# Attention-state scan with a gated MLP on one core: late steps in another order, a 128-row identity product, U in pairs

## The chip, the cores and the metric

One core of a Trainium2 chip. The time is that of the device for one execution, in microseconds; the median of several runs counts. Engines: TensorE (PE, with its weight loads as PEld), VectorE (DVE), ScalarE (ACT), GpSimd (POOL), SyncE (SP), which issues most DMAs. Each engine runs its own queue in order and waits on semaphores of the others.

## What is computed

For each of 4 batches and 8 heads a 40x40 state runs over 768 tokens; the outputs are joined and go through a gated MLP. Cut to what matters:

```python
for t in range(S):
    y[:, :, t] = einsum('bhd,bhde->bhe', rt, state)
    Sa = einsum('bhde,bhe->bhd', state, at)
    state = state * wt - outer(Sa, bt) + outer(vt, kt)
x = y with the heads joined                    # 4 x 768 x 320
h = relu(x @ w_in); u, v = halves of h         # 512 columns each
v = normalized over its 512 columns
out = (u * (w_spatial @ v + b_spatial)) @ w_out
```

All is float32. The matrices of the MLP are split into two parts, a high one and a rest, so one product becomes three.

## The kernel before, in words

**Two phases.** `phase1` does the scan and, beside it, the first layer of the MLP; `phase2` does the spatial product (L179 to L181) and the last product (L199). In phase 1 the tokens go in chunks of 64. There are 24 steps (`NS`): two pairs of batches, 12 chunks each; a step handles 2 batches by 8 heads, that is 8 units (`NU`) in two groups `g` of 4, each unit with two heads (`par`) in partitions 0 to 39 and 64 to 103.

**What a step does.** Ahead of it: the scans of the decays (`scan1`, `scan2`, L287 to L296, tiles S and Et), `at_mul` and `sl_mul` (L315, L321), `lprime` (L336, products of 64x32), and for four steps at once `invert` (L352 to L374), which inverts triangular blocks on VectorE in 30 pairs of L363 and L367 and ends with two transposes, XT (L372) and X (L374). Then `b_lka` (L393, tile lk), `b_h` (L419), `b_tok` (L435, transposes), `b_l21` (L453), `b_zt` (L471), `b_x21` (L498) build what does not depend on the state. The chain through the state, for each group: `c_bp` (L529: state Mc by the late inputs, into bp), `c_own` (L545) and `c_far` (L554) into the PSUM bank ch, `c_xx` (L569), then `c_mp` (L597 and L603), from which VectorE makes the next Mc (L614), and `c_y` (L625), from which it makes y (L638). ScalarE evicts nearly every product from PSUM; GpSimd then sets the upper triangle of lk and Rt to zero (L402, called selects here). `c_mp` adds Mc through an identity: L597 multiplies 40 rows of `ident` (an identity of 128) by 40 rows of Mc, once for each `par`, and L603 adds the rest with 128 rows and 40 columns of weights.

**The MLP's first layer.** Twelve blocks of 128 tokens for a pair of batches: `m_load` reads x back from DRAM, `m_split` makes the high part (ScalarE) and the rest (L55, GpSimd: xl and a part of xh), then in slots `m_u` (L746: 8 products of 256 columns; 4 slots a block) and `m_v` (L696: 8 of 512; 2 slots). A slot writes the one bank `pv` (behind step 23, in turn, also `itmp`); ScalarE evicts it (L751, L701); v is normalized (L707 to L735); both go to DRAM.

**What sets the order.** A list of times. `at(t, fn, ...)` puts a call at a time counted in steps; the list is sorted, and all that stands before 24 is issued in just that order, each engine taking its own instructions from it. Steps 0 to 10 take their times from `CE`, `REG`, `LEAD` and `FIRST`; from `S1` = 11 on (the late steps) from `CH`, `RL` and `LL`, where the two groups run half a step apart: the L569 rounds of one group alternate with L529 of the other, and L554 with L545. `PREP`, `GAP`, `LPQ` and `OV` set the loads, scans and `lprime`, `INV_T` the inversions, `T_DEC` the decoding of the weights. `MS` gives the slots of a late step, four of them; calls behind 24 are left to the framework's scheduler, together with phase 2.

**Tile shapes.** A product takes a part of TensorE's 128x128 array that its rows and columns of weights set: 64x64 for L393, L419, L453, L529, L545, L554, L569 and L597; 64x32 for L336; 32x32 for L471 and L498; 128x64 for L603 and L625; 128x128 for L435, L696 and L746.

Of the kernel before, what the change touches and what calls it, by code (L numbers as in the profile page):

```python
# [216 lines left out]
def phase1(ctx, tc, early, late, vtok, win, xs, vns, uts, dscr):  # L217
# [520 lines left out]
    def m_u(d, bq, i, k=0):  # L738
        xh, xl = st["xhl", (bq, i)]
        dc = slice(d * P, (d + 1) * P)  # L740
        pu = m_ps(k)[:, 0:NB * P].rearrange("p (g t) -> p g t", g=NB)
        mm = [(wh[:, k, dc], xh[:, k]) for k in range(3)]
        mm += [(wh[:, k, dc], xl[:, k]) for k in range(2)]
        mm += [(wl[:, k, dc], xh[:, k]) for k in range(3)]
        for j, (l, r) in enumerate(mm):
            nc.tensor.matmul(pu, lhsT=l, rhs=r, start=(j == 0), stop=(j == len(mm) - 1))  # L746
        st["pu", d] = pu

    def m_u_out(d, bq, i):
        ur = st["act"].tile([P, NB, P], F32, name="ur", bufs=2)  # L750
        nc.scalar.activation(ur, st["pu", d], AF.Relu)  # L751
        nc.sync.dma_start(out=uts[bq, i, d], in_=ur)
# [43 lines left out]
    REG = dict(lka=-0.02, lka_out=0.02, tok=0.4, tok_out=0.43, l21=0.52, l21_out=0.54, zt=0.66, zt_out=0.68, h=0.68, h_out=0.72, x=0.5, x21=0.78, x21_out=0.81, dt=0.03)  # L796
# [1 line left out]
    RL = dict(REG, lka=0.16, lka_out=0.2, tok=0.66, tok_out=0.72, l21=0.32, l21_out=0.33, zt=0.46, zt_out=0.47, h=0.27, h_out=0.29, x=0.73, x21=0.78, x21_out=0.8, dt=0.03)
    LL = dict(RL, zt=0.88, zt_out=0.90, x=0.975, x21=1.12, x21_out=1.16)
    FIRST = dict(REG, tok=0.37, tok_out=0.375, l21=0.45, l21_out=0.452, zt=0.47, zt_out=0.5, x=0.7, h=0.8, h_out=0.81, x21=0.65, x21_out=0.71)  # L800
# [212 lines left out]
```

## Time and profile before

| | |
|---|---|
| runs | 679.25 us median of 3 (673.93 to 680.66) |
| profiled execution | 676.05 us; span 674.3 us |
| busy over the span | PE 597.7, PEld 533.3, DVE 446.1, ACT 327.1, POOL 268.4 us |
| DMA | 81.47 MB, 121 GB/s |
| step 12 begins | 281.7 us; step 23 at 485.1 us |

A profile's time is the one execution's; the span runs from the first instruction to the last. Busy time counts instructions at work, and matmul ends are modelled. Steps are told here by the first L529 of their group 0. A late step is 17 to 22 us long, an early one 15 to 31.

### The profile page before, as it was taken

The page shows a single profiled execution, that of the slowest core. Times are in us where ns is not written, and L with a number is a line of the kernel's source. Part 1 is how long each engine was busy: PE and PEld are TensorE (multiplying, and loading weights), DVE is VectorE, ACT ScalarE, POOL GpSimd, SP SyncE. Part 2 cuts the span into 40 slices and gives each one's busy share as a digit, 9 for nine tenths or more (in the row PEclk, how much of TensorE's full clock was granted, in tenths as well). Part 3 has the DMA queues.
Part 4 walks back from the last instruction along what each step waited for, and adds up shares of the span by engine and source line. Part 5 has one row for each costly group of instructions (what it writes and reads, how often), then busy time and mean ns, then how long its engine had stood idle before and what let it go on. Part 6 is the DMA issues. An engine that isn't in the chain of part 4 may idle for free.

```text
span 674.3 us, 27090 instructions
## 1 busy us (share of the span) xinstructions
PE 597.7 (89%) x11728; PEld 533.3 (79%) x11728; DVE 446.1 (66%) x951; ACT 327.1 (49%) x719; POOL 268.4 (40%) x381
## 2 busy tenths in 40 slices
PE   1538986699888989998999999999898999999998
PEld 1427875588777878887887888888687999999997
DVE  8898789965999999778885576534285662232221
ACT  2214552235655645765666666676564543232122
POOL 3102440223534535545454344453353645352221
PEclk9975996756998998999999999999998999999999
DMA  8812553262545444453545444444265567150001
GB/s 199 153 38 54 139 156 98 78 145 55 146 106 133 130 109 132 128 145 107 138 124 159 106 119 121 130 135 139 84 208 182 159 187 222 33 184 30 29 31 59
DMA packets 106208, 81.47 MB, mean 121 GB/s; under 512 B 34984, under 2 KB 91560, under 8 KB 105896
## 3 DMA queue, kind: packets, MB, share of 16 engines
q1 hardware_dynamic: 105544, 78.02, 42.0%
q10 hardware_dynamic: 544, 1.72, 1.1%
q8 instruction: 92, 1.51, 0.9%
q14 instruction: 28, 0.23, 0.1%
HBM read 59.20 MB, written 20.50 MB: 118 GB/s over the span
## 4 chain that ended last, share of the span: by engine, by line
PE 62%; DVE 22%; DMA 6%; issue 3%; POOL 3%; ACT 2%; SPq 1%; DVEq 0%; POOLq 0%; ACTq 0%
PE po L199 6%; PE pv L746 5%; PE pv L696 5%; DVE itmp L363 4%; PE pg L181 4%; PE ch L569 4%; PE pg L180 4%; PE pg L179 4%; DVE A L367 4%; PE ch L554 3%; PE bp L625 3%; PE bk L435 3%; PE bk L419 2%; DMA ein<-in_early 2%; PE ch L545 2%
## 5 line engine op out<-in xcount | busy, mean ns | idle before, releaser
L402 POOL TENSOR_SCALAR_AFFINE_SELECT Rt<-Rt 64x512 f32<-64x512 f32 (+1 forms) x144 | 85.7, 597 | 153.0 <-ACT Rt L585 128.8
L402 POOL TENSOR_SCALAR_AFFINE_SELECT lk<-lk 64x512 f32<-64x512 f32 x48 | 46.8, 976 | 109.5 <-ACT lk L410 108.3
L363 DVE TENSOR_TENSOR itmp<-A 128x30 f32<-128x30 f32 (+9 forms) x180 | 70.6, 392 | 2.9
L183 DVE TENSOR_TENSOR g<-pg,bb 128x384 f32<-128x384 f32 x32 | 17.8, 557 | 80.0 <-PE pg L181 74.4
L179 PE MATMUL pg<-wsh,vh 128*128 128x384 f32 x192 | 65.4, 341 | 0.4 <-ACT vh L51 0.4
L180 PE MATMUL pg<-wsl,vh 128*128 128x384 f32 x192 | 65.1, 339 | 0.0
L181 PE MATMUL pg<-wsh,vl 128*128 128x384 f32 x192 | 63.8, 336 | 0.0
L367 DVE TENSOR_TENSOR A<-A,itmp 128x30 f32<-128x30 f32 (+9 forms) x180 | 59.0, 328 | 6.1
L545 PE MATMUL ch<-Rt,lk 64*64 64x104 f32 x768 | 48.9, 270 | 13.0 <-issue 9.1
L55 POOL TENSOR_TENSOR gl<-g,gh 128x384 fp32r<-128x384 f32 x32 | 33.3, 1045 | 60.5 <-ACT gh L51 60.5
L585 ACT ACTIVATE Rt<-ch 64x416 f32<-64x416 f32 x96 | 49.2, 512 | 14.5 <-PE ch L569 6.4
L545 PEld LDWEIGHTS ch<-Rt,lk 64*64 64x64 f32 x768 | 40.5, 144 | 15.8 <-issue 10.7
L529 PE MATMUL bp<-lin,Mc 40*64 40x104 f32 x768 | 46.8, 268 | 4.2 <-DVE y L638 4.2
L554 PE MATMUL ch<-Bt,at 40*64 40x104 f32 x768 | 47.6, 270 | 0.3 <-ACT Bt L536 0.3
L614 DVE TENSOR_TENSOR Mc<-ch,scn 104x160 f32<-104x160 f32 x44 | 18.6, 435 | 43.7 <-PE ch L603 34.4
L569 PE MATMUL ch<-ffs,xf 64*64 64x104 f32 x768 | 46.6, 269 | 0.1
L55 POOL TENSOR_TENSOR vl<-raw,vh 128x512 fp32r<-128x512 f32 x24 | 31.7, 1327 | 32.9 <-ACT vh L51 30.3
L529 PEld LDWEIGHTS bp<-lin,Mc 40*64 40x64 f32 x768 | 39.5, 144 | 5.1 <-DVE y L638 5.1
L554 PEld LDWEIGHTS ch<-Bt,at 40*64 40x64 f32 x768 | 38.8, 144 | 4.1 <-issue 1.8
L569 PEld LDWEIGHTS ch<-ffs,xf 64*64 64x64 f32 x768 | 39.1, 144 | 3.0 <-issue 1.1
L51 ACT ACTIVATE gh<-g 128x384 fp32r<-128x384 f32 x32 | 16.6, 519 | 50.6 <-DVE g L184 50.6
L336 PE MATMUL bk<-at,sl 64*32 64x32 f32 x1536 | 22.1, 212 | 21.2 <-DVE sl L321 19.8
(132 smaller groups left out, 1582.1 us busy)
## 6 DMA issues: line engine op xcount, KB each, us to landing
lin<-in_late SPq DMA_DIRECT2D x48, 160.0 KB
ein<-in_early SPq DMA_DIRECT2D x36, 192.0 KB
uts<-ur SPq DMA_DIRECT2D x48, 128.0 KB
vns<-vr SPq DMA_DIRECT2D x24, 256.0 KB
raw<-vns SPq DMA_DIRECT2D x24, 256.0 KB
ut<-uts SPq DMA_DIRECT2D x24, 256.0 KB
...
```

What stands on the lines that cost most here:

```text
L55: eng.tensor_tensor(out=lo, in0=x, in1=hi.bitcast(F32), op=ALU.subtract)
L179: nc.tensor.matmul(pg, lhsT=vh[:, dc], rhs=w_h, start=(i == 0), stop=False)
L180: nc.tensor.matmul(pg, lhsT=vh[:, dc], rhs=w_l, start=False, stop=False)
L181: nc.tensor.matmul(pg, lhsT=vl[:, dc], rhs=w_h, start=False, stop=(i == NT - 1))
L363: nc.vector.tensor_tensor(out=tp, in0=A[:, k + 1:, k:k + 1].broadcast_to([P, m, k]), in1=A[:, k:k + 1, 0:k].broadcast_to([P, m, k]), op=AL ...
L367: nc.vector.tensor_tensor(out=A[:, k + 1:, 0:k], in0=A[:, k + 1:, 0:k], in1=tp, op=ALU.add)
L402: nc.gpsimd.affine_select(out=t, in_=t, pattern=[[0, k], [1, C]], base=0, channel_multiplier=-1, compare_op=ALU.is_gt, fill=0.0,)
L529: nc.tensor.matmul(st["bp", g][PR[par], q, :], lhsT=Mc[RR[par], n, :], rhs=li[RR[par], n, C:], start=(q == 0), stop=False, skip_group_chec ...
L545: nc.tensor.matmul(st["ff", g][ev, q, :], lhsT=st["lk", s][ev, n, :], rhs=Rts[s % 2][par][ev, n, :], start=(q == 0), stop=False, skip_grou ...
L554: nc.tensor.matmul(st["ff", g][PR[1 - par], q, :], lhsT=at[RR[par], n, :], rhs=st["Bt", g][RR[par], q, :], start=False, stop=True, skip_gr ...
L569: nc.tensor.matmul(st["xx", g][PR[1 - half], q, :], lhsT=xfs[s % 2][ev, n, :], rhs=st["ffs", g][ev, q, :], start=True, stop=True,)
L585: done = nc.scalar.activation(Rt[par][PR[par], gp], xx[PR[par]], AF.Copy, scale=-1.0)
```

## The change

1. `c_mp`: the identity product takes all 128 rows of `ident` and Mc, with the same 40 columns.
2. `m_u`: two blocks of U (256 columns each) are computed in one slot, side by side in the 512 columns of a bank; one eviction takes both; the two stores stay. A block has 4 slots now, U pair, V, U pair, V. `ur` doubles; `xt` has 1 buffer (2 before), `vr` 2 (3), `l21` 2 (1).
3. `MS` has three slots a step, and `CH`, `RL`, `LL` give the late steps another order.
4. Ahead of step 11 `REG`, `FIRST`, `PREP`, `GAP`, `INV_T`, `T_DEC` and `OV` are changed in some places: zt's eviction from 0.68 to 0.77; the scans of step 5 earlier by 0.22 and of steps 6 and 16 to 21 later by 0.04 to 0.08; the second inversion's end from 3.7 to 3.78. `m_load` comes at 1.5 steps before its block's first slot (3.2 before), `m_split` at 0.9 (0.75).

```diff
-        l21 = jat.tile([P, NU, HB], F32, name="l21", bufs=1)
+        l21 = jat.tile([P, NU, HB], F32, name="l21", bufs=2)
...
-                mp[rows], lhsT=ident[rows, rows], rhs=Mc[rows, gp, 0:E],
+                mp[rows], lhsT=ident[:, rows], rhs=Mc[:, gp, 0:E],
...
-    def m_u(d, bq, i, k=0):
+    def m_u(h, bq, i, k=0):
         xh, xl = st["xhl", (bq, i)]
+        pu = m_ps(k).rearrange("p (d g t) -> p d g t", d=2, g=NB)
+        for d in range(2):
+            dc = slice((2 * h + d) * P, (2 * h + d + 1) * P)
...
+                nc.tensor.matmul(
+                    pu[:, d], lhsT=l, rhs=r, start=(j == 0), stop=(j == len(mm) - 1), skip_group_check=True,
+                )
...
+        ur = st["act"].tile([P, 2, NB, P], F32, name="ur", bufs=2)
+        nc.scalar.activation(ur, st["pu", h], AF.Relu)
+        for d in range(2):
+            nc.sync.dma_start(out=uts[bq, i, 2 * h + d], in_=ur[:, d])
...
-    MS = (0.02, 0.34, 0.52, 0.82)
-    CH = dict(far=0.25, bp_out=0.035, ff_out=0.255, xx=0.5, xx_out=0.52, mp=0.64, mp_out=0.645, y=0.76, y_out=0.77, store=0.9)
+    MS = (0.02, 0.52, 0.78)
+    CH = dict(far=0.25, bp_out=0.035, ff_out=0.255, xx=0.5, xx_out=0.52, mp=0.6, mp_out=0.605, y=0.62, y_out=0.63, store=0.9)
...
-        own = slots[6 * j:6 * j + 6]
-        at(max(own[0] - 3.2, 2 * j + 2.5, T_DEC[5] + 7 * 0.1 + 0.02), m_load, bq, i)
-        at(max(own[0] - 0.75, 2 * j + 2.9), m_split, bq, i)
+        own = slots[4 * j:4 * j + 4]
+        at(max(own[0] - 1.5, 2 * j + 2.5, T_DEC[5] + 7 * 0.1 + 0.02), m_load, bq, i)
+        at(max(own[0] - 0.9, 2 * j + 2.9), m_split, bq, i)
```

TensorE, the second half of late step 14, before: from the last L529 beside L569 to the next L569. A row is a line, an operation, out<-in, the output's shape and a count; L746 are U products, L696 V products.

```order
L529 MATMUL bp_5942<-lin_136,Mc 64x104 x2
L696 MATMUL pv<-wh,xh 128x512 x3
...
L597 MATMUL ch_5939<-Mc,ident 40x4x40 x2
L603 MATMUL ch_5939<-tk,Rt_132 40x40
...
L435 MATMUL bk<-ident,sl 128x128 x8
L554 MATMUL ch_5821<-Bt,at 64x104 x2
L545 MATMUL ch_6018<-Rt_134,lk 64x104
...
L625 MATMUL bp_5738<-Rt_132,tk 40x64
...
L498 MATMUL bk<-zt,X_4767 32x32 x16
L746 MATMUL pv<-xh,wh 128x256 x3
...
L336 MATMUL bk<-at,sl 32x32 x32
L569 MATMUL ch_6129<-ffs,xf_130 64x104 x2
```

The same place of the changed kernel, where U products are L747:

```order
L529 MATMUL bp_5921<-lin_136,Mc 64x104 x2
L747 MATMUL pv<-xh,wh 128x256 x3
...
L435 MATMUL bk<-ident,sl 128x128 x8
L597 MATMUL ch_5918<-Mc,ident 40x4x40 x2
L603 MATMUL ch_5918<-tk,Rt_132 40x40
...
L625 MATMUL bp_5740<-Rt_132,tk 40x64
...
L554 MATMUL ch_5842<-Bt,at 64x104 x2
L545 MATMUL ch_6019<-Rt_134,lk 64x104
...
L453 MATMUL bk<-sl,at 64x32 x16
L696 MATMUL pv<-wh,xh 128x512 x3
...
L336 MATMUL bk<-at,sl 32x32 x32
...
L569 MATMUL ch_6140<-ffs,xf_130 64x104 x2
```

L625 moved from behind L554 and L545 to directly behind L603; L435 stands ahead of L597, behind the MLP's products; a U slot has 16 products. In the step's first half L393 and L419 now stand between L554 and L569.

VectorE at the end of the second inversion, which serves steps 4 to 7, before; S, Et, at and sl belong to the scans of step 11.

```order
L287 SCALAR_TENSOR_TENSOR S<-ein_124,ends 128x528
L291 RECIPROCAL ends<-S 128x8
L372 STREAM_TRANSPOSE XT_1957<-A 128x32x32
L374 STREAM_TRANSPOSE X_1958<-A 128x32x32
L296 SCALAR_TENSOR_TENSOR Et<-ein_124,ends 128x528
L315 TENSOR_TENSOR at<-ein_124,Et 128x512
L321 TENSOR_TENSOR sl<-ein_124,S 128x1024
L614 TENSOR_TENSOR Mc<-ch_1914,scn 104x4x40
L614 TENSOR_TENSOR Mc<-ch_1930,scn 104x4x40
L638 TENSOR_TENSOR y_1641<-bp_1732,Et 104x4x64
```

And of the changed kernel, from the inversion's last L367:

```order
L367 TENSOR_TENSOR A<-A,itmp 128x30
L296 SCALAR_TENSOR_TENSOR Et<-ein_124,ends 128x528
L372 STREAM_TRANSPOSE XT_1984<-A 128x32x32
L315 TENSOR_TENSOR at<-ein_124,Et 128x512
L321 TENSOR_TENSOR sl<-ein_124,S 128x1024
L614 TENSOR_TENSOR Mc<-ch_1911,scn 104x4x40
L614 TENSOR_TENSOR Mc<-ch_1924,scn 104x4x40
L374 STREAM_TRANSPOSE X_1985<-A 128x32x32
L638 TENSOR_TENSOR y_1638<-bp_1729,Et 104x4x64
```

X (L374) moved behind the two Mc; XT (L372) stands behind Et, and the last pairs of the inversion stand behind S.

GpSimd in two late steps, before: the split of a block of x (L55) among the selects. The Rt of 8x64 belong to `b_h`, those of 4x64 to `c_xx`.

```order
L402 AFFINE_SELECT lk<-lk 64x512 x2
L55 TENSOR_TENSOR xl<-xt,xh 128x512
L55 TENSOR_TENSOR xh<-xt,xh 64x256
L402 AFFINE_SELECT Rt_132<-Rt_132 64x8x64
L402 AFFINE_SELECT Rt_133<-Rt_133 64x8x64
L402 AFFINE_SELECT Rt_134<-Rt_134 64x4x64
L402 AFFINE_SELECT Rt_135<-Rt_135 64x4x64
L487 COPY xf_130<-XT_7804 128x8x32
L489 COPY xf_130<-XT_7804 32x8x32 x2
L402 AFFINE_SELECT Rt_134<-Rt_134 64x4x64
```

And in a place of the changed kernel:

```order
L402 AFFINE_SELECT lk<-lk 64x512 x2
L402 AFFINE_SELECT Rt_134<-Rt_134 64x8x64
L402 AFFINE_SELECT Rt_135<-Rt_135 64x8x64
L402 AFFINE_SELECT Rt_132<-Rt_132 64x4x64
L402 AFFINE_SELECT Rt_133<-Rt_133 64x4x64
L487 COPY xf_131<-XT_7840 128x8x32
L489 COPY xf_131<-XT_7840 32x8x32 x2
L55 TENSOR_TENSOR xl<-xt,xh 128x512
L55 TENSOR_TENSOR xh<-xt,xh 64x256
L402 AFFINE_SELECT Rt_132<-Rt_132 64x4x64
L402 AFFINE_SELECT Rt_133<-Rt_133 64x4x64
L402 AFFINE_SELECT lk<-lk 64x512 x2
```

The split moved from between lk and Rt of `b_h` to the place behind the copies of XT, directly ahead of two selects of `c_xx` (those of a step's first half). In phase 1 four of its splits stand so, in the kernel before four as well.

## Rows read from the trace of the kernel before

**Rows 1.** The page, part 1: busy us (share of the span) xinstructions.

```profile
PE 597.7 (89%) x11728; PEld 533.3 (79%) x11728; DVE 446.1 (66%) x951; ACT 327.1 (49%) x719; POOL 268.4 (40%) x381
```

**Rows 2.** Stretches, steps 14 to 21: length, busy of each engine, clock, DMA, GB/s.

```profile
376.45:393.51 17.06, 17.06 (x404) 14.39 (x403) 10.81 (x32) 11.93 (x25) 6.30 (x12) 1.00 0.35 92
...
sum 143.15, PE 141.42 PEld 118.40 DVE 91.17 ACT 94.84 POOL 64.99; mean PE 17.68 PEld 14.80 DVE 11.40 ACT 11.86 POOL 8.12
```

**Rows 3.** TensorE in order of time, step 12 into 13: start us, us, instruction, xcount.

```profile
291.35 0.31 PE L569 MATMUL ch<-ffs,xf 64*64 64x104 f32 x2
...
291.49 0.26 PE L569 MATMUL ch<-ffs,xf 64*64 64x104 f32 x2
...
292.02 0.26 PE L569 MATMUL ch<-ffs,xf 64*64 64x104 f32 x2
...
292.22 0.62 PE L746 MATMUL pv<-xh,wh 128*128 128x256 f32 x3
292.68 0.40 PE L746 MATMUL pv<-xl,wh 128*128 128x256 f32 x2
292.92 0.52 PE L746 MATMUL pv<-xh,wl 128*128 128x256 f32 x3
293.43 0.47 PE L597 MATMUL ch<-Mc,ident 40*40 40x160 f32 x4
293.83 0.51 PE L603 MATMUL ch<-tk,Rt 128*40 128x40 f32 x16
294.26 1.09 PE L435 MATMUL bk<-ident,sl 128*128 128x128 f32 x8
...
296.16 0.65 PE L625 MATMUL bp<-Rt,tk 128*40 128x64 f32 x16
296.74 0.69 PE L498 MATMUL bk<-zt,X 32*32 32x32 f32 x32
...
300.15 0.98 PE L696 MATMUL pv<-wh,xh 128*128 128x512 f32 x3
...
302.22 0.47 PE L597 MATMUL ch<-Mc,ident 40*40 40x160 f32 x4
```

**Rows 4.** Stretches, early steps, the same columns as in rows 2.

```profile
100.00:150.00 50.00, 37.06 (x730) 33.08 (x732) 41.90 (x79) 14.25 (x33) 10.11 (x21) 0.63 0.43 108
```

**Rows 5.** TensorE's weight loads in order of time.

```profile
292.56 0.30 PEld L746 LDWEIGHTS pv<-xl,wh 128*128 128x128 f32 x2
```

**Rows 6.** VectorE in order of time, steps 12 and 13.

```profile
294.44 0.44 DVE L614 TENSOR_TENSOR Mc<-ch,scn 104x160 f32<-104x160 f32 x1 [0.15 <-PE ch L603]
...
314.89 0.43 DVE L614 TENSOR_TENSOR Mc<-ch,scn 104x160 f32<-104x160 f32 x1
```

**Rows 7.** TensorE in order of time, step 13, with [idle before <-releaser].

```profile
315.42 0.40 PE L545 MATMUL ch<-Rt,lk 64*64 64x104 f32 x3 [1.92 <-POOL xf L489]
```

**Rows 8.** GpSimd's groups, steps 14 to 21: xcount | busy us, mean ns | idle before.

```profile
L402 POOL TENSOR_SCALAR_AFFINE_SELECT lk<-lk 64x512 f32<-64x512 f32 x16 | 16.4, 1027 | 19.9 <-ACT lk L410 19.5
L402 POOL TENSOR_SCALAR_AFFINE_SELECT Rt<-Rt 64x256 f32<-64x256 f32 x32 | 14.7, 459 | 42.1 <-ACT Rt L585 40.2
L402 POOL TENSOR_SCALAR_AFFINE_SELECT Rt<-Rt 64x512 f32<-64x512 f32 x16 | 12.7, 791 | 3.9 <-ACT Rt L428 3.4
L55 POOL TENSOR_TENSOR xl<-xt,xh 128x512 fp32r<-128x512 f32 x5 | 7.4, 1485 | 9.5 <-issue 9.3
...
L55 POOL TENSOR_TENSOR xh<-xt,xh 64x256 fp32r<-64x256 f32 x5 | 3.7, 738 | 0.4
```

**Rows 9.** VectorE in order of time, end of the second inversion.

```profile
128.86 1.99 DVE L374 STREAM_TRANSPOSE X<-A 128x1024 f32<-128x1024 f32 x1
130.70 1.27 DVE L296 TENSOR_TENSOR_SCAN Et<-ein,ends 128x528 f32<-128x528 f32 x1
```

**Rows 10.** TensorE in order of time, before step 4.

```profile
134.33 0.53 PE L545 MATMUL ch<-Rt,lk 64*64 64x104 f32 x2 [2.40 <-issue]
```

**Rows 11.** TensorE in order of time, behind step 23.

```profile
515.06 0.62 PE L746 MATMUL pv<-xh,wh 128*128 128x256 f32 x3 [2.06 <-ACT ur L751]
```

More of the change, by code (lines that the diff above doesn't have):

```diff
@@ L665, in m_load @@
         ts = slice(i * P, (i + 1) * P)
-        xt = st["act"].tile([P, 3, NB, P], F32, name="xt", bufs=2)
+        xt = st["act"].tile([P, 3, NB, P], F32, name="xt", bufs=1)
         for g in range(NB):
@@ L699, in m_v_out @@
     def m_v_out(g):
-        vr = st["act"].tile([P, DH], F32, name="vr", bufs=3)
+        vr = st["act"].tile([P, DH], F32, name="vr", bufs=2)
         nc.scalar.activation(vr, st["pv", g], AF.Relu)
@@ L736, in m_n3, with m_u_out @@
         nc.sync.dma_start(out=vns[bq * NB + g, i], in_=vr)
-    def m_u(d, bq, i, k=0):
+    def m_u(h, bq, i, k=0):
         xh, xl = st["xhl", (bq, i)]
[L740 to L752, printed above, removed]
+        pu = m_ps(k).rearrange("p (d g t) -> p d g t", d=2, g=NB)
+        for d in range(2):
+            dc = slice((2 * h + d) * P, (2 * h + d + 1) * P)
+            mm = [(wh[:, k, dc], xh[:, k]) for k in range(3)]
+            mm += [(wh[:, k, dc], xl[:, k]) for k in range(2)]
+            mm += [(wl[:, k, dc], xh[:, k]) for k in range(3)]
+            for j, (l, r) in enumerate(mm):
+                nc.tensor.matmul(
+                    pu[:, d], lhsT=l, rhs=r, start=(j == 0), stop=(j == len(mm) - 1), skip_group_check=True,
+                )
+        st["pu", h] = pu
+    def m_u_out(h, bq, i):
+        ur = st["act"].tile([P, 2, NB, P], F32, name="ur", bufs=2)
+        nc.scalar.activation(ur, st["pu", h], AF.Relu)
+        for d in range(2):
+            nc.sync.dma_start(out=uts[bq, i, 2 * h + d], in_=ur[:, d])
     plan = []
@@ L795, in phase1 @@
                 at(s + (CE[k] + GE.get(k, 0.05) * g if s < S1 else CH[k] + 0.50 * g), fn, s, g)
[L796 removed]
+    REG = dict(lka=-0.02, lka_out=0.02, tok=0.4, tok_out=0.43, l21=0.52, l21_out=0.54, zt=0.66, zt_out=0.77, h=0.68, h_out=0.72, x=0.5, x21=0.78, x21_out=0.81, dt=0.03)
     LEAD = dict(REG, zt=0.88, zt_out=0.90, x=0.975, x21=1.12, x21_out=1.16)
[L798 to L800 removed]
+    RL = dict(REG, lka=0.27, lka_out=0.29, tok=0.56, tok_out=0.58, l21=-0.23, l21_out=-0.225, zt=0.95, zt_out=0.955, h=0.31, h_out=0.33, x=0.73, x21=1.2, x21_out=1.21, dt=0.003)
+    LL = dict(RL)
+    FIRST = dict(REG, tok=0.37, tok_out=0.375, l21=0.45, l21_out=0.452, zt=0.47, zt_out=0.5, x=0.7, h=0.8, h_out=0.855, x21=0.65, x21_out=0.71)
     for q in range(1, NS):
@@ L847, in phase1 @@
             at(t0 + (t1 - t0) * k / (INV_N - 1), step, gen)
-    T_DEC, T_MOE = (4.2, 5.2, 6.2, 7.2, 8.2, 9.2), 11
+    T_DEC, T_MOE = (4.12, 5.2, 6.2, 7.2, 8.2, 9.12), 11
     for i in range(6):
@@ L855, in phase1 @@
     slots = []
-    for k in range(3 * NS):
-        slots.append(max(T_MOE + k // len(MS) + MS[k % len(MS)], 2 * (k // 6) + 3.12 + 0.07 * (k % 6)))
+    for k in range(2 * NS):
+        slots.append(max(T_MOE + k // len(MS) + MS[k % len(MS)], 2 * (k // 4) + 3.12 + 0.07 * (k % 4)))
     def tail(t):
@@ L863, in phase1 @@
         bq, i = j // 6, j % 6
-        own = slots[6 * j:6 * j + 6]
-        at(max(own[0] - 3.2, 2 * j + 2.5, T_DEC[5] + 7 * 0.1 + 0.02), m_load, bq, i)
-        at(max(own[0] - 0.75, 2 * j + 2.9), m_split, bq, i)
-        for t, d in zip((own[0], own[1], own[3], own[4]), range(DH // P)):
-            at(t, m_u, d, bq, i, tail(t))
-            at(t + 0.04, m_u_out, d, bq, i)
-        for t, g in zip((own[2], own[5]), range(NB)):
+        own = slots[4 * j:4 * j + 4]
+        at(max(own[0] - 1.5, 2 * j + 2.5, T_DEC[5] + 7 * 0.1 + 0.02), m_load, bq, i)
+        at(max(own[0] - 0.9, 2 * j + 2.9), m_split, bq, i)
+        for h in range(2):
+            t = own[2 * h]
+            at(t, m_u, h, bq, i, tail(t))
+            at(t + 0.04, m_u_out, h, bq, i)
+        for t, g in zip((own[1], own[3]), range(NB)):
             at(t, m_v, g, bq, i, tail(t))
```

8 lines of the change are left out of this document (4 added, 4 removed).

## The prediction

> **What bounds the kernel now.** I read the busy shares on the page first: TensorE works for 597.7 of the 674.3 us, far ahead of the next engine [rows 1]. That is an average, so the second view is the table of stretches, one stretch for each late step. There TensorE's busy time is the step itself: 17.06 of 17.06 us in the step from 376.45, and 141.42 of 143.15 us over eight steps, while VectorE, ScalarE and GpSimd have 91, 95 and 65 us [rows 2]. The granted clock is 1.00, the 2.4 GHz level. So a late step takes as long as its products, and the question is what these spend.
>
> The third view, TensorE's instructions in order of time, answers that. In a row of products with the same tile shape (the L569 and L529 products, four at a time), six rounds pass from 291.49 to 292.02, 0.088 us each. But the first round takes 0.14 us (291.35 to 291.49), and after the last one, at 292.02, the next product, of another shape, starts only at 292.22: 0.20 us in place of 0.088 [rows 3]. So a visit to a shape costs 0.05 at its start and 0.11 at its end beyond the products. At L746 two products take 0.24 (292.68 to 292.92) and the first three 0.46, not 0.36, so its start costs 0.10; with an end of about 0.09 that is 0.19 [rows 3]. I take 0.16 us for a change of shape, with 0.11 (the end alone) and 0.19 as its bounds.
>
> **The change part by part.** The time of each part is set against the profiled execution, 676.05 us (span 674.3, 1.75 around it). It lies 3.2 us under the median of the three runs, 679.25, within their spread of 6.7; less than 1%, 6.8 us, cannot be told from no change here.
>
> *Order of the late steps and U in pairs.* I count shapes in TensorE's order: 64x64 (L393, L419, L453, L529, L545, L554, L569, and L597 before), 64x32 (L336), 32x32 (L471, L498), 128x64 (L603, L625, and L597 after), 128x128 (L435 and the U and V products). From the middle of step 11 to the end of step 23 there are 219 runs of one shape before and 129 after. TensorE's order rows above show half a step of it: L597, L603 and L625 become one run, and L435 joins the run of the U pair. 90 runs fewer by 0.16 is -14.4 us (0.11: -9.9; 0.19: -17.1). The number of products, their columns and hence the rest of their time stay. MoE work moves: three slots in a step, two blocks of U or one of V in each, replace four single ones, so a step takes in more of it and the tail that much less; on a TensorE that is full in both places this adds nothing.
>
> *Identity product.* It takes 0.40 us for its four records (293.43 to 293.83) [rows 3]. With 128 rows it has L603's shape; by the 104 columns that a round streams in 0.088, 160 columns take 0.135, two rounds 0.27. It saves 0.13 a group. The 22 late groups are in the 90. The other 22, in steps 0 to 10, come to 2.9 us; there VectorE is as busy as TensorE or busier (41.90 against 37.06 of 50 us from 100 on) [rows 4], so I count half: -1.4 (0 to -2.9).
>
> A rule of the chip could speak against it. On the rows first: the loads for two L746 products, which use all 128 rows, start at 292.56 [rows 5], while the products before them run until 292.84 (292.22 plus 0.62) [rows 3]. The Trainium skill, TensorE: Matmul & The Clock Gate, section Part 3: Packing small matmuls, has it that a weight load overlaps a running product only where the row groups differ; by that the four identity loads, now on all rows, would stand bare. The trace disagrees: by its rows the sum is 663, by the rule it would be 682 (rival 3).
>
> *U eviction.* One eviction of 512 columns stands for two of 256. ScalarE is idle a third of these steps [rows 2], so nothing is gained on the path. The price would be a TensorE that waits for the bank: the next slot comes behind L453, L471 or the L569 round, never at once. Zero.
>
> *Loads of x.* With one `xt` buffer the load of a block, issued by SyncE, waits for the split of the block before, and SyncE's later DMAs (lin, vtok, the early pieces) queue behind it. Blocks are 4 slots, 1.33 steps, apart; the load comes 1.5 and the split 0.9 steps ahead of the first slot, so that split is planned 0.73 step, some 12 us, before the load that needs it. Zero; without that lead a step would wait for the split's 2.22 us [rows 8] about every 1.33 steps, which lies in the bound of the selects below.
>
> *A wait that grows.* L545 of the next step writes the bank that mp has filled, so it waits until VectorE has read it (L614). At 293.83 mp starts, L614 runs from 294.44 to 294.88 [rows 3, 6], and L545 can start 0.10 later, as behind the L614 that ends at 315.32 (315.42) [rows 6, 7]. Before, L393 or L435 stands between (L435 starts at 294.26). Now, in a step's second half, only y (L625) does, 0.58 us with its end (296.16 to 296.74) [rows 3]. Without the shape's end y starts at about 294.15, so L545 is reached at 294.73 and held to 294.98: 0.25 us in each of 12 steps, +3.0. The lower bound is 0. For the upper one I let a late VectorE, which cost 1.92 at 315.42 [rows 7], strike in four of the twelve: +10.7. What queues behind L545 are all of TensorE's products. I take 3.0, since 16 of the 22 late L614 start within 0.15 us of mp's end, as the first one at 294.44 does.
>
> *Selects on GpSimd.* y needs the selects of Rt. A split of x (1.485 and 0.738 us) stands directly ahead of the two selects (0.459 each) of a step's first half four times [rows 8]. y now comes 2.66 us after the L569 rounds (a V, 300.15 to 302.22, and mp with 0.27 and 0.32, the latter 293.83 to 294.26 less an end of 0.11) against 3.94 in the half step of the rows (292.22 to 296.16) [rows 3]. So it may wait; 0 to 2.22 in each, +8.9 at most; I take 1.5, nearer to 0, as four splits stood so before too, and no wait of TensorE from 300 to 500 us was at y.
>
> *The plan ahead of step 11.* VectorE's order at the end of the second inversion now has Mc (L614) before the transpose X (L374, 128.86 to 130.70, 1.84 us), while XT comes one scan (1.27) later [rows 9]. L545 of step 4 waited 2.40 us for that L614, from 131.93 to 134.33 [rows 10]. Freed 1.84 earlier, it is held by the products ahead of it, which wait for XT and reach it at 133.20: -1.1 (0 to -1.8). Other moves there (zt's eviction behind h's, loads a tenth of a step) lie beside VectorE's queue: 0.
>
> *Tail.* Nine slots in place of 20 remain behind step 23. TensorE waited 2.06 us there for an eviction [rows 11]. With half the slots I count -1.0 (0 to -2.1).
>
> Sum: -14.4 -1.4 +3.0 +1.5 -1.1 -1.0 = -13.4; 676.05 - 13.4 is 662.65, say 663. All lower ends give 652, all upper ones 686.
>
> **Rivals.**
> 1. New waits take the place of the old ends: L545 and the selects at half of what their upper bounds add (+3.9 and +3.7), and shape ends at 0.11 (+4.5): 663 + 12.1 = 675. For it: everything that hid a wait on TensorE gets shorter, and VectorE is at 91 of 143 us. Against it: only 1.7 of the 143 were idle [rows 2].
> 2. Slower. In the second half GpSimd now gets lk, Rt and the xx selects in one sequence: 2 x 1.027, 2 x 0.791, 2 x 0.459 is 4.55 us [rows 8], from L393's end to y, with evictions before and between. TensorE needs 4.6 in that time for the L569 rounds (0.87), a V (2.07), L435 (1.09) and mp (0.59) [rows 3], and L419 besides. If evictions, hops and other work put GpSimd 2.4 us behind that, y holds all of TensorE in 12 steps: +28.8, 691. It decides from 1.1 us a step on (13.4 in 12). Against it: with L419 there is slack, and half the evictions lie beside GpSimd's own time.
> 3. The identity product gains nothing because its loads stand bare. By the loads at 292.56, 0.30 for two [rows 5], four cost 0.6: with 22 late groups and half of the 22 early ones +19.8, 682. The rule weighed above would do this. Against it stand the L746 loads [rows 5].
> 4. The identity product in its new form still ends its own run: 44 groups keep 0.13, 22 of them half hidden, +4.3: 667.
> 5. More is gained: waits that TensorE had between the late steps go too, and the stretch from 100 to 150 us, where the granted clock is at 0.63 [rows 4], finds it higher. With all lower ends, 652.
>
> **How the numbers follow.** Forecast 0.67, rival 1 0.12, rival 2 0.04, rival 3 0.02, rival 4 0.04, rival 5 0.11. Within 1% of 679.25 is 672.5 to 686. Faster: 0.67 + 0.04 + 0.11 and a sixth of rival 1, 0.84. Slower: rival 2, 0.04. The same: the remainder, 0.12. The range goes from 649, below rival 5 by what the runs spread, to 676, just past rival 1; rivals 2 and 3, and little else, lie outside.
>
> **What would show it.** Right: late steps of 16.3 to 17 us at full clock; L597 followed by L603 at the pace of one run; L625 directly behind L603; L545 with a short idle time behind L614 in second halves only. Wrong: L625 with idle time ended by a select on GpSimd (rival 2), L545 held for over 1 us in many steps (rival 1), L597 loads that start after the product before them has ended (rival 3), or late steps as long as before with no idle time, which would mean that a change of shape is not what the 0.20 us were.

## The result and the profile after

The changed kernel takes 657.91 us, the median of 4 runs (656.5 to 662.05), against 678.19 us for the kernel before (4 runs, 673.93 to 680.66): a ratio of 0.9718, 95% interval 0.965 to 0.9785. On another chip the ratio is 0.9784 (0.968 to 0.9889). Medians are over all runs and ratios leave disturbed runs out, so a ratio need not be that of its medians. The profiled execution, against which the prediction made its sum, took 662.05 us, 14.0 less than that of before (676.05); its mean granted clock was 0.938, that of the other three 0.948 to 0.961.

The page, busy times over a span of 660.3 us, as in [rows 1]:

```profile
PE 581.3 (88%) x11728; PEld 532.5 (81%) x11728; DVE 442.6 (67%) x951; ACT 322.3 (49%) x695; POOL 268.7 (41%) x381
```

TensorE has as many products as before and works 16.4 us less. Where that went is read from the table of stretches, cut at the first L529 of step 12 and of step 23. Columns: start and end, length, busy time of each engine, clock, DMA share, GB/s. First the kernel before:

```profile
281.70:485.08 203.38, 198.13 (x4685) 165.32 (x4679) 128.18 (x323) 132.54 (x289) 94.74 (x148) 1.00 0.45 127
485.08:674.20 189.12, 181.92 (x1245) 175.45 (x1244) 74.84 (x163) 67.33 (x143) 73.73 (x68) 0.99 0.39 120
sum 392.50, PE 380.05 PEld 340.77 DVE 203.02 ACT 199.87 POOL 168.47; mean PE 190.03 PEld 170.38 DVE 101.51 ACT 99.93 POOL 84.24
```

Then the changed kernel:

```profile
280.26:478.12 197.86, 191.53 (x4661) 169.02 (x4655) 133.07 (x340) 130.64 (x280) 87.86 (x147) 1.00 0.50 139
478.12:660.20 182.08, 172.97 (x1232) 167.52 (x1228) 65.42 (x147) 63.33 (x130) 72.14 (x66) 1.00 0.39 120
sum 379.94, PE 364.50 PEld 336.54 DVE 198.50 ACT 193.96 POOL 160.00; mean PE 182.25 PEld 168.27 DVE 99.25 ACT 96.98 POOL 80.00
```

So 1.4 us went ahead of step 12, 5.5 in the late steps and 7.0 behind them. From step 12 on TensorE's busy time falls by 15.55 us (380.05 to 364.50), and its idle time grows by 3.0 (392.50 - 380.05 = 12.45, 379.94 - 364.50 = 15.44). The prediction had -14.4 and +3.5 for these two.

Not all of the 15.55 us is the order's. Two parts come off. First, some work has moved ahead of step 12: from there on the trace has 360 U products before and 352 after, and 352 products of L453 before and 320 after. At 0.12 us for a U product and 0.85 us for the 32 of L453 (both read from rows below) that is 1.8 us. Second, behind step 23 the kernel before ran for 3.4 us at half the clock:

```profile
515.90:519.30 3.40, 3.40 (x13) 3.12 (x12) 1.11 (x5) 3.34 (x6) 2.75 (x3) 0.50 0.26 88
```

Its products of 384 columns start 0.33 us apart there (518.55 to 518.88) and 0.17 us apart right behind it (519.61 to 519.78), so this cost some 1.7 us; the changed kernel's profile has no such fall between step 12 and the end of its products. Some 12.0 us of busy time are left for the order, the U pairs and the identity product.

A late step, as in [rows 2] (steps 20 and 22, and the sum of steps 17 to 22):

```profile
425.73:442.51 16.78, 16.78 (x406) 14.73 (x402) 6.07 (x19) 11.60 (x26) 5.32 (x11) 1.00 0.53 144
...
459.89:478.12 18.23, 18.23 (x383) 15.33 (x379) 8.45 (x21) 11.91 (x26) 8.03 (x13) 1.00 0.39 113
sum 104.41, PE 103.46 PEld 91.36 DVE 60.07 ACT 70.71 POOL 44.45; mean PE 17.24 PEld 15.23 DVE 10.01 ACT 11.79 POOL 7.41
```

Still TensorE's busy time is the step. These six steps, in which the granted clock is 1.00 in every run, are the yardstick of the experiments: 104.41 us here, 108.63 before (376.45 to 485.08).

TensorE in order of time, step 18, as in [rows 3]:

```profile
399.06 0.26 PE L569 MATMUL ch<-ffs,xf 64*64 64x104 f32 x2
399.25 0.63 PE L747 MATMUL pv<-xh,wh 128*128 128x256 f32 x3
...
400.90 0.52 PE L747 MATMUL pv<-xh,wl 128*128 128x256 f32 x3
401.27 1.03 PE L435 MATMUL bk<-ident,sl 128*128 128x128 f32 x8
402.23 0.47 PE L597 MATMUL ch<-Mc,ident 128*40 128x160 f32 x4
402.53 0.47 PE L603 MATMUL ch<-tk,Rt 128*40 128x40 f32 x16
402.83 0.62 PE L625 MATMUL bp<-Rt,tk 128*40 128x64 f32 x16
```

The U pair takes 2.02 us and runs into L435 without an end of its own; L597 takes 0.30 (402.23 to 402.53) where it took 0.40; L603 and L625 follow at the pace of one run.

### The profile page after: what moved, and what is told of

Its sections match the earlier page's. It is cut to its first block, busy times and chain, and to the rows that moved or that the text cites. A ratio compares the mean times of both kernels' runs of the same rounds, so it can differ in the third digit from the quotient of the medians.

```text
span 660.3 us, 27038 instructions
## 1 busy us (share of the span) xinstructions
PE 581.3 (88%) x11728; PEld 532.5 (81%) x11728; DVE 442.6 (67%) x951; ACT 322.3 (49%) x695; POOL 268.7 (41%) x381
## 4 chain that ended last, share of the span: by engine, by line
PE 60%; DVE 16%; DMA 9%; ACT 5%; issue 4%; POOL 3%; SPq 2%; ACTq 0%; DVEq 0%
PE po L199 6%; PE pv L747 5%; PE pv L696 5%; PE pg L179 4%; PE pg L180 4%; PE pg L181 4%; PE ch L569 4%; PE ch L554 4%; DVE itmp L363 4%; DVE A L367 3%; DMA ein<-in_early 3%; PE bk L453 3%; PE bp L625 3%; PE ch L545 2%; PE bk L435 2%
## 5 line engine op out<-in xcount | busy, mean ns | idle before, releaser
L402 POOL TENSOR_SCALAR_AFFINE_SELECT lk<-lk 64x512 f32<-64x512 f32 x48 | 37.9, 790 | 114.9 <-ACT lk L410 108.4
L363 DVE TENSOR_TENSOR itmp<-A 128x30 f32<-128x30 f32 (+9 forms) x180 | 72.1, 400 | 3.0
L367 DVE TENSOR_TENSOR A<-A,itmp 128x30 f32<-128x30 f32 (+9 forms) x180 | 59.0, 328 | 6.1
L55 POOL TENSOR_TENSOR gl<-g,gh 128x384 fp32r<-128x384 f32 x32 | 33.6, 1053 | 54.9 <-ACT gh L51 54.9
L545 PE MATMUL ch<-Rt,lk 64*64 64x104 f32 x768 | 48.1, 267 | 7.7 <-issue 3.8
L614 DVE TENSOR_TENSOR Mc<-ch,scn 104x160 f32<-104x160 f32 x44 | 18.8, 440 | 50.0 <-PE ch L603 31.3
L529 PE MATMUL bp<-lin,Mc 40*64 40x104 f32 x768 | 47.0, 264 | 3.2 <-DVE y L638 2.7
L554 PE MATMUL ch<-Bt,at 40*64 40x104 f32 x768 | 49.4, 277 | 0.5 <-ACT Bt L536 0.5
L569 PE MATMUL ch<-ffs,xf 64*64 64x104 f32 x768 | 49.0, 279 | 0.6 <-ACT ffs L561 0.6
L545 PEld LDWEIGHTS ch<-Rt,lk 64*64 64x64 f32 x768 | 39.4, 142 | 10.1 <-issue 4.8
L569 PEld LDWEIGHTS ch<-ffs,xf 64*64 64x64 f32 x768 | 41.8, 152 | 2.1 <-ACT ffs L561 1.2
L554 PEld LDWEIGHTS ch<-Bt,at 40*64 40x64 f32 x768 | 39.9, 147 | 3.4 <-ACT Bt L536 1.5
L529 PEld LDWEIGHTS bp<-lin,Mc 40*64 40x64 f32 x768 | 38.5, 139 | 4.2 <-DVE y L638 3.5
L55 POOL TENSOR_TENSOR vl<-raw,vh 128x512 fp32r<-128x512 f32 x24 | 32.6, 1366 | 21.1 <-ACT vh L51 16.9
L336 PE MATMUL bk<-at,sl 64*32 64x32 f32 x1536 | 20.8, 205 | 22.7 <-DVE sl L321 20.3
```

Source lines behind the costliest of these rows:

```text
L55: eng.tensor_tensor(out=lo, in0=x, in1=hi.bitcast(F32), op=ALU.subtract)
L363: nc.vector.tensor_tensor(out=tp, in0=A[:, k + 1:, k:k + 1].broadcast_to([P, m, k]), in1=A[:, k:k + 1, 0:k].broadcast_to([P, m, k]), op=AL ...
L367: nc.vector.tensor_tensor(out=A[:, k + 1:, 0:k], in0=A[:, k + 1:, 0:k], in1=tp, op=ALU.add)
L402: nc.gpsimd.affine_select(out=t, in_=t, pattern=[[0, k], [1, C]], base=0, channel_multiplier=-1, compare_op=ALU.is_gt, fill=0.0,)
L529: nc.tensor.matmul(st["bp", g][PR[par], q, :], lhsT=Mc[RR[par], n, :], rhs=li[RR[par], n, C:], start=(q == 0), stop=False, skip_group_chec ...
L545: nc.tensor.matmul(st["ff", g][ev, q, :], lhsT=st["lk", s][ev, n, :], rhs=Rts[s % 2][par][ev, n, :], start=(q == 0), stop=False, skip_grou ...
```

## The experiments

Theory: from step 12 on the time is TensorE's, and each change of tile shape costs it some 0.16 us. Rivals: the gain is the clock's or the early plan's; it comes from something else in the change than the order of the products; the waits set the time. A ratio is always against the kernel before on the same chip. Three chips were used: one for the changed kernel again, the identity product undone, the early plan alone and L453 ahead; one for the added products, the old order and three vr buffers; one for the other four.

**The changed kernel again.** No edit.

> The changed kernel once more, so that the runs beside it can be compared on one chip. Every theory: 0.97 of the kernel before, 656 to 662 us; in the second half of each late step L545 is held 0.2 to 0.25 us behind L614.

656.91 us, ratio 0.9784 (0.968 to 0.9889); its six steps took 104.01 us, the stretch behind step 23 180.5.

**The identity product, undone and alone.**

```diff
-                mp[rows], lhsT=ident[:, rows], rhs=Mc[:, gp, 0:E],
+                mp[rows], lhsT=ident[rows, rows], rhs=Mc[rows, gp, 0:E],
```

> The changed kernel with the identity product back on 40 rows. Theory (each change of tile shape costs some 0.16 us of a full TensorE, and the time follows their number): 22 more runs of one shape from the middle of step 11 to the end of step 23, +3.5 us, and 0 to +2.9 in the early steps: +3.5 to +6.4 over the changed kernel, 661 to 664 us. Rival (weight loads on all 128 rows stand bare, those on 40 rows beside other rows don't): faster than the changed kernel, by up to 19 us. Rival (the gain of the change came from elsewhere, the clock or the plan ahead of step 11): within 1 us of the changed kernel.

663.96 us, ratio 0.9866 (0.9752 to 0.9981), against 656.91 for the changed kernel on this chip. The two intervals overlap, and the profiled executions took 662.00 and 662.45, so the 7 us between the medians can't be put down to the edit. The sum of steps 17 to 22, by the same stretches:

```profile
sum 105.82, PE 104.93 PEld 90.22 DVE 59.88 ACT 70.73 POOL 44.06; mean PE 104.93 PEld 90.22 DVE 59.88 ACT 70.73 POOL 44.06
```

TensorE is busy 1.47 us longer than the 103.46 of the changed kernel, in 12 groups: 0.12 each. The other way round, the identity edit alone in the kernel before:

> The kernel before with the identity product alone on 128 rows. Theory (a change of shape costs 0.11 to 0.16 us, the identity product joins L603's run): 12 groups between steps 17 and 23 by 0.13 us, that stretch 1.6 us shorter than the 108.63 us of before; over the kernel -3 us in the late steps and 0 to -3 in the early ones. Rival (weight loads on 128 rows stand bare): that stretch 7 us longer, the kernel 16 us slower.

678.49 us, ratio 0.9991 (0.9941 to 1.0042): by the time nothing can be told. By the six steps it can:

```profile
sum 107.36, PE 105.57 PEld 90.03 DVE 57.38 ACT 70.98 POOL 47.67; mean PE 105.57 PEld 90.03 DVE 57.38 ACT 70.98 POOL 47.67
```

1.27 us less than 108.63, 0.11 a group (in TensorE's busy time 107.04 - 105.57 = 1.47, as in the run before). Loads on 128 rows don't stand bare in either kernel that has them: rival 3 would have added 7 us here. TensorE's weight loads in the changed kernel, step 20:

```profile
436.86 0.16 PEld L597 LDWEIGHTS ch<-Mc,ident 128*40 128x40 f32 x4 [0.17 <-ACT ur L754]
437.03 0.49 PEld L603 LDWEIGHTS ch<-tk,Rt 128*40 128x40 f32 x16
```

The loads for L603, on all rows, begin at 437.03, while the L597 products, on all rows too, run until L603's first at 437.17. The Trainium skill, TensorE: Matmul & The Clock Gate, section Part 3: Packing small matmuls, has in its list of what overlaps that a weight load overlaps running products only where the row groups differ; this trace doesn't agree (437.03 against 437.17). The prediction took 0.16 for each of the late groups; the direct price is a quarter to a third lower.

**The price of a change of shape by itself.** Four products more in each U pair, between products of its first block. U is changed by them; everything else is left.

```diff
+                if d == 0 and j in (1, 3, 4, 5):
+                    nc.tensor.matmul(
+                        pu[0:64, 1, 0, 0:64], lhsT=wh[0:64, 0, 0:64], rhs=xh[0:64, 0, 0, 0:64], start=True, stop=True,
+                        skip_group_check=True,
+                    )
```

> The changed kernel with four more products in each of the 24 U pairs, each between two of the first block's products, with 64 rows and 64 columns of weights and 64 streamed columns; their result is overwritten by the second block. So 192 more changes of shape. Theory: 192 by 0.16 us, +31 us (0.11: +21, 0.19: +36), beside what the products themselves take, which the run with 128-row products shows. Rival (a change of shape costs nothing of its own, the 0.20 us in the trace are a pipeline end that other products cover): the same time as that run, to 3 us.

686.07 us, ratio 1.0099 (1.0049 to 1.0148). TensorE in order of time, one U pair of step 19; L751 are the added products:

```profile
412.96 0.50 PE L747 MATMUL pv<-xh,wh 128*128 128x256 f32 x2
413.39 0.24 PE L751 MATMUL pv<-xh,wh 64*64 64x64 f32 x1
413.56 0.38 PE L747 MATMUL pv<-xh,wh 128*128 128x256 f32 x1
413.78 0.28 PE L747 MATMUL pv<-xl,wh 128*128 128x256 f32 x1
...
416.43 1.03 PE L435 MATMUL bk<-ident,sl 128*128 128x128 f32 x8
```

The control has `pu[:, 1, 0, 0:64]`, `wh[:, 0, 0:128]` and `xh[:, 0, 0, 0:64]` in these products:

> The same four products in each U pair, but with 128 rows and 128 columns of weights, the shape of the products around them: no change of shape. All theories: 96 products of 64 columns, 0.03 us each by their columns or up to 0.12 by the pace of L747: +3 to +12 us over the changed kernel.

666.11 us, ratio 0.9834 (0.9792 to 0.9875). The same place:

```profile
410.70 0.50 PE L747 MATMUL pv<-xh,wh 128*128 128x256 f32 x2
411.05 0.19 PE L751 MATMUL pv<-xh,wh 128*128 128x64 f32 x1
411.08 0.36 PE L747 MATMUL pv<-xh,wh 128*128 128x256 f32 x1
411.27 0.28 PE L747 MATMUL pv<-xl,wh 128*128 128x256 f32 x1
...
412.79 0.52 PE L747 MATMUL pv<-xh,wl 128*128 128x256 f32 x3
```

With the 64-row products the pair takes 3.47 us (412.96 to 416.43), 1.45 more than 2.02: 0.36 for each. A product of 64 columns holds TensorE for 0.03 us when it has the shape of its neighbours (411.05 to 411.08). The other 0.33 are two changes of shape: 0.165 each. In the six steps the difference of the two kernels is 115.71 - 106.65 = 9.06 us for 72 changes, 0.126 each; that is less because an added 128-row product also delays the one behind it (0.19 us, 411.08 to 411.27, instead of 0.12). The rival, the same time for both, is out: 20.0 us lie between the medians. For the 192 changes of the whole kernel that is 0.10 us each, under the 0.11 to 0.19 expected; what the pairs outside the six steps cost by themselves is not shown.

**The old order of the late steps in the changed kernel.**

```diff
-    CH = dict(far=0.25, bp_out=0.035, ff_out=0.255, xx=0.5, xx_out=0.52, mp=0.6, mp_out=0.605, y=0.62, y_out=0.63, store=0.9)
+    CH = dict(far=0.25, bp_out=0.035, ff_out=0.255, xx=0.5, xx_out=0.52, mp=0.64, mp_out=0.645, y=0.76, y_out=0.77, store=0.9)
...
-    RL = dict(REG, lka=0.27, lka_out=0.29, tok=0.56, tok_out=0.58, l21=-0.23, l21_out=-0.225, zt=0.95, zt_out=0.955, h=0.31, h_out=0.33, x=0.73, x21=1.2, x21_out=1.21, dt=0.003)
+    RL = dict(REG, lka=0.16, lka_out=0.2, tok=0.66, tok_out=0.72, l21=0.32, l21_out=0.33, zt=0.46, zt_out=0.47, h=0.27, h_out=0.29, x=0.73, x21=0.78, x21_out=0.8, dt=0.03)
...
```

> The changed kernel (U pairs, three slots a step, 128-row identity, the other early plan) with the late steps in the order of before (CH, RL, LL; l21 with one buffer again). TensorE's order has 188 runs of one shape from the middle of step 11 to the end of step 23, against 135 in the changed kernel and 223 before. Theory (0.16 us for each run): +8.5 us over the changed kernel (0.11: +5.8, 0.19: +10), to be found in the steps from 12 on. Rival (the U pairs and the plan ahead of step 11 bring the gain, the order of the products nothing): within 2 us of the changed kernel.

673.82 us, ratio 0.9998 (0.996 to 1.0035): nothing is left of the gain, about 14 us (span 674.6 against 660.3) where the theory had 8.5. TensorE, the sum of steps 17 to 22, and a wait that stands there four times:

```profile
388.83 0.54 PE L471 MATMUL bk<-XT,l 32*32 32x32 f32 x22 [0.67 <-ACT l L461]
...
sum 109.96, PE 107.29 PEld 92.82 DVE 62.74 ACT 72.48 POOL 48.16; mean PE 107.29 PEld 92.82 DVE 62.74 ACT 72.48 POOL 48.16
```

In these six steps busy time grows by 3.83 us, of which 0.85 are 32 L453 products that the changed kernel has outside them: 3.0 for 28 changes of shape, 0.11 each. Idle time grows by 1.7: nothing stands between L453 and L471 there, and L471 waits for ScalarE's l21. From step 12 to the end:

```profile
280.46:674.60 394.14, 376.17 (x5918) 343.59 (x5912) 201.91 (x489) 198.30 (x411) 163.24 (x213) 0.99 0.42 125
```

Against the 379.94 us of the changed kernel (step 12 begins within 0.2 us of it) that is 14.2 more: 2.5 of idle time and 11.7 of busy time. Of the latter 0.85 are L453 again. Up to 5.2 are the clock's: this execution ran 10.3 us at a granted clock of 0.50 (336.6 to 340.0, 507.3 to 510.7 and 524.3 to 527.7), the profiled one of the changed kernel none. The 5.7 that are left stand for 53 changes of shape, 0.11 each, against the theory's 8.5. So the theory's part is there, at its lower bound. Whether the old order's waits bring on the lower clock is not shown.

**L453 ahead of the second half's L554 and L545.**

```diff
-    RL = dict(REG, lka=0.27, lka_out=0.29, tok=0.56, tok_out=0.58, l21=-0.23, l21_out=-0.225, zt=0.95, zt_out=0.955, h=0.31, h_out=0.33, x=0.73, x21=1.2, x21_out=1.21, dt=0.003)
+    RL = dict(REG, lka=0.27, lka_out=0.29, tok=0.56, tok_out=0.58, l21=-0.255, l21_out=-0.252, zt=0.95, zt_out=0.955, h=0.31, h_out=0.33, x=0.73, x21=1.2, x21_out=1.21, dt=0.003)
```

> The changed kernel with L453 (64x64, as L554 and L545) moved ahead of the L554 and L545 products of the second half, so that more TensorE work stands between the reading of Mc's bank and L545; as many changes of shape as in the changed kernel. Theory (the wait of L545 for L614 is on the path, 0.22 us in 11 steps): -2.4 us against the changed kernel, L545 without idle time in second halves. Rival (what is late then is something else, such as GpSimd's selects or the eviction Bt that L554 reads): within 0.5 us of the changed kernel, the idle time found at another line.

656.56 us against 656.91. TensorE in order of time in the changed kernel, second half of step 20:

```profile
437.17 0.47 PE L603 MATMUL ch<-tk,Rt 128*40 128x40 f32 x16
437.47 0.62 PE L625 MATMUL bp<-Rt,tk 128*40 128x64 f32 x16
438.02 0.40 PE L554 MATMUL ch<-Bt,at 40*64 40x104 f32 x4
438.24 0.31 PE L545 MATMUL ch<-Rt,lk 64*64 64x104 f32 x2
...
438.84 0.26 PE L453 MATMUL bk<-sl,at 64*64 64x32 f32 x4
438.92 0.25 PE L545 MATMUL ch<-Rt,lk 64*64 64x104 f32 x2
...
439.84 0.96 PE L696 MATMUL pv<-wh,xh 128*128 128x512 f32 x3
```

And with L453 ahead:

```profile
435.56 0.47 PE L603 MATMUL ch<-tk,Rt 128*40 128x40 f32 x16
...
436.41 1.06 PE L453 MATMUL bk<-sl,at 64*64 64x32 f32 x30
437.26 0.31 PE L545 MATMUL ch<-Rt,lk 64*64 64x104 f32 x2
...
438.20 0.96 PE L696 MATMUL pv<-wh,xh 128*128 128x512 f32 x3
```

The wait is gone, and it was worth next to nothing: from L603 to the V products 2.67 us with it, 2.64 without. It is the same in the other steps from 17 to 22 (2.68 against 2.65), but for step 18. While L545 waits (0.22 us, 438.02 to 438.24) the L554 products of the same rounds run, in other quarters of the array, and at the end L453 starts in the quarters that L554 has left (438.84) while the last L545 (438.92) still runs. The six steps took 103.22 us, 1.2 less than 104.41 and 0.8 less than the 104.01 of the changed kernel's second profile; nearly all of the 1.2 is in steps 18 and 19 (16.76 for 17.41, 16.80 for 17.22). In step 18 VectorE came to L614 late (the row at 404.24 below); what step 19 lost is not shown. The other four differ by 0.05 us or less. Neither 2.4 us nor another wait in its place: the time was not lost in the first place.

**The early plan, alone and undone.** Only the tables REG, FIRST, PREP, GAP, INV_T, OV and T_DEC are exchanged, in the kernel before:

```diff
-    INV_T = {1: (2.5, 3.7), 2: (4.5, 7.7), 3: (8.1, 11.7), 4: (12.1, 15.7), 5: (16.1, 19.7)}
+    INV_T = {1: (2.5, 3.78), 2: (4.5, 7.7), 3: (8.1, 11.7), 4: (12.06, 15.78), 5: (16.1, 19.7)}
...
-    T_DEC, T_MOE = (4.2, 5.2, 6.2, 7.2, 8.2, 9.2), 11
+    T_DEC, T_MOE = (4.12, 5.2, 6.2, 7.2, 8.2, 9.12), 11
...
```

> The kernel before with only the other plan ahead of step 11 (the tables REG, FIRST, PREP, GAP, INV_T, OV and T_DEC). Theory: 0 to -1.5 us against the kernel before, within what can be told, step 12 beginning 0 to 1.5 us sooner. Rival (the early plan or the clock that it meets brought most of the gain): -8 us or more.

678.41 us, ratio 1.0091 (1.0035 to 1.0147). And the same lines the other way in the changed kernel:

> The changed kernel with the plan ahead of step 11 of before (REG, FIRST, PREP, GAP, INV_T, OV, T_DEC), the late order, the U pairs and the identity product kept. Theory (the early plan is worth next to nothing): within 2 us of the changed kernel. Rival (the early plan lets the changed kernel meet a higher clock ahead of step 12, and that is where the medians gained more than the profiles): 5 us or more over the changed kernel, with step 12 beginning later than 283 us.

660.29 us, ratio 0.983 (0.9745 to 0.9915). The changed kernel itself was not run on this chip; with both small edits (below) it took 659.19 there. Step 12 began at 285.08 us in the first and at 271.12 in the second, the opposite of the rival. The clock differs between executions. The stretch ahead of step 12, of the early plan alone:

```profile
0.00:285.08 285.08, 216.98 (x5810) 191.42 (x5810) 244.22 (x466) 127.73 (x287) 106.07 (x166) 0.86 0.46 115
```

of the changed kernel with three vr buffers (below):

```profile
0.00:272.09 272.09, 205.15 (x5850) 183.76 (x5850) 245.32 (x465) 127.41 (x287) 107.70 (x168) 0.97 0.49 119
```

and of the second profile of the kernel before, all three stretches:

> The kernel before once more, for a second profile. All theories: step 12 to 23 203 us, the stretch behind step 23 189 us, as in the first profile, to 1 us; the start of step 12 tells how far the part ahead of it differs from one execution to the next.

```profile
0.00:276.49 276.49, 208.93 (x5810) 184.71 (x5811) 243.32 (x466) 127.59 (x287) 101.82 (x166) 0.88 0.47 119
276.49:484.67 208.18, 202.66 (x4685) 169.15 (x4679) 128.17 (x323) 132.64 (x289) 94.38 (x148) 0.98 0.44 124
484.67:672.80 188.13, 181.46 (x1245) 175.73 (x1244) 75.22 (x163) 67.42 (x143) 73.49 (x68) 0.99 0.39 121
```

The kernel before begins step 12 at 281.70 in one execution and at 276.49 in another; the clock is 0.84 to 0.97, VectorE's busy time 243 to 245 us in these three. The clock alone doesn't order the starts: step 12 begins at 271.12 with 0.89 (the early plan undone) and at 272.09 with 0.97. A gain of 1 or 2 us there can't be told. If anything the early plan costs time: alone it was 0.9% slower, with an interval that leaves out 1. The miss of this expectation is the 203 us: steps 12 to 16 also meet a lower clock in some executions (0.98 over the stretch), and it took 208; steps 17 to 22 took 108.61 again.

**Three vr buffers.**

```diff
-        vr = st["act"].tile([P, DH], F32, name="vr", bufs=2)
+        vr = st["act"].tile([P, DH], F32, name="vr", bufs=3)
```

> The changed kernel with three vr buffers again. In the changed kernel ScalarE stands 3.1 us at L701 behind the store of an older vr, and TensorE 2.64 us behind that at L696 (494.28 us). Theory (two vr buffers are a new wait of the change): that wait goes, -2 to -3.3 us behind step 23 against the changed kernel. Rival (the next late thing takes its place): less than 1 us.

655.66 us, ratio 0.9686 (0.9625 to 0.9748). The wait at L696 is gone, and another stands a little behind it:

```profile
499.99 0.50 PE L747 MATMUL pv<-xh,wh 128*128 128x256 f32 x2 [2.55 <-ACT ur L754]
```

The stretch behind step 23 took 180.6 us, against 182.2 and 180.5 in the changed kernel's two profiles. By these numbers the rival is right, but it isn't settled: this run stood at a granted clock of 0.50 for 3.4 us there (from 500.6), worth up to 1.7 us, and the changed kernel's two profiles didn't.

**Both small edits together.**

> The changed kernel with three vr buffers and with L453 ahead of the L554 and L545 products of the second half, the two edits that took a wait away in runs of their own. Theory: steps 17 to 23 as in the run with L453 ahead (103.2 us, some 1 us less than the changed kernel), and the stretch behind step 23 no longer than its 182 us: 0.5 to 2 us less than the changed kernel in all, too little to be told from it by times.

659.19 us, ratio 0.9861 (0.979 to 0.9932); six steps 103.54 us, behind them 181.1, again with 3.4 us at 0.50. No version here is faster than the changed kernel by what a run can tell.

## Why the prediction came out right

*The order and U in pairs, -14.4.* Right in mechanism and inside its bounds, but some 2.4 us too large. TensorE is busy 15.55 us less from step 12 on, and 12.0 of that are left when the moved work and the clock come off. By the trace it has 88 runs of one shape fewer there (64x64: 82 to 38, 128x128: 61 to 39, 128x64: 47 to 25): 0.14 us each where the prediction took 0.16. The six steps give 0.14 too (next paragraph). Measured by itself a change costs 0.13 to 0.165. Where the identity product joined L603's run, 0.11 to 0.12 with its shorter streaming included.

*The length of a late step, 16.3 to 17 us.* Wrong: 16.8 to 18.2 in steps 17 to 22. The prediction had it that "a step takes in more of it and the tail that much less", and the step that failed is that the length it gave left this out. Records of the six steps, grouped by line, before and after: the L746 products `xh,wh`, three to a block, are 48 and the L747 ones 54, the L696 products `wh,xh` into `pv`, three to a V, 24 and 27. So two U blocks and one V of twice their size more: four times about 0.96 us, +3.85. With the 0.85 of L453 the other way, 107.04 + 3.0 - 103.46 is 6.6 us for 46 runs fewer (109 to 63), 0.14 each; only 4.2 show as time of the steps, because they do more of the MLP; the work that they took over is missing behind step 23 (-7.0, of which 1.7 are the clock's).

*L545 behind L614, +3.0.* The wait came as worked out (0.22 us foreseen as 0.25, second halves only). Its price did not: 0.03. The step that failed is "What queues behind L545 are all of TensorE's products": the L554 products ahead of it were still running, and L453 behind it could start beside it.

*Waits that did come.* TensorE in order of time in the changed kernel, with the idle time before and what ended it:

```profile
132.98 1.06 PE L471 MATMUL bk<-XT,l 32*32 32x32 f32 x32 [6.43 <-DVE XT L372]
...
310.03 0.30 PE L625 MATMUL bp<-Rt,tk 128*40 128x64 f32 x2 [0.43 <-POOL Rt L402]
...
358.04 0.73 PE L696 MATMUL pv<-wh,xh 128*128 128x512 f32 x2 [2.31 <-issue]
...
404.24 0.31 PE L545 MATMUL ch<-Rt,lk 64*64 64x104 f32 x2 [0.46 <-DVE Mc L614]
...
494.28 0.73 PE L696 MATMUL itmp<-wh,xh 128*128 128x512 f32 x2 [2.64 <-ACT vr L701]
```

Between steps 12 and 23 the selects held L625 seven times, 1.8 us in all where 1.5 was taken (0.43 and 0.50 the longest); rival 2 asked for 2.4 in every step. VectorE was late for L545 twice (0.49 and 0.46) and for L336 once (1.14, at 353.06), and the longest, 2.31, has no releaser. So the +3.0 of idle time agrees with the prediction's sum and not with its places: 1.1 of it are in the steps, where 4.5 were foreseen, and 1.9 behind them, where -1.0 was.

*Tail, -1.0.* Wrong in sign: TensorE's idle time behind step 23 grew from 7.2 to 9.1 us. The wait of [rows 11] is gone, and a new one stands at 494.28. ScalarE there:

```profile
493.63 0.60 ACT L701 ACTIVATE vr<-itmp 128x512 f32<-128x512 f32 x1 [3.10 <-DMA vns<-vr]
```

With two vr buffers the eviction waits for the store of an older one. The change's text named `vr` 2 (3); the prediction put no price on it, and that is the step that failed. In the run with three buffers another wait, 2.55 us, followed; what the third buffer is worth stays open within some 2 us, because of the clock there.

*The early plan, -1.1, and early identity groups, -1.4.* Not shown, and for the plan the runs speak against it. The wait that was to shrink has another end: XT, which the plan puts later, holds L471 for 6.43 us (the row at 132.98 above). Before, L471 waited less:

```profile
129.15 0.69 PE L471 MATMUL bk<-XT,l 32*32 32x32 f32 x32 [3.73 <-DVE XT L372]
```

With the 2.40 at L545 [rows 10] that was 6.13 us; now it is 6.43 at L471 and none at L545. The step that failed is that XT comes one scan, 1.27 us, later: it starts at 130.95 for 127.12, and 1.45 of these 3.8 us are there from step 3 on (107.22 for 105.77). Step 4 starts at 138.31 for 137.13. The whole stretch ahead of step 12 differs by up to 14 us between executions.

*U eviction and loads of x, zero.* No wait of TensorE over 0.3 us between steps 12 and 23 ends at either. *Rivals.* The first came in part, by other waits (3 us of idle time in all); the second, third and fourth not; of the fifth only the clock, which differs from one execution to the next.

*The total.* 662.65 was the sum for the profiled execution, which took 662.05. That the two lie 0.6 us apart is luck: the order brought 2.4 us less than taken and L545 cost nothing, but 1.8 us of work moved ahead of step 12, 1.7 us were the clock's in the kernel before, and waits came where none were priced. By the medians the gain is 20.3 us, by the ratio on the second chip some 15, by the profiled executions 14.0; the other three executions took 656.5 to 657.93 at mean granted clocks of 0.948 to 0.961, and no trace shows where these gained.
